# In a gated attention-plus-GLU kernel, the last down-projection job gets one PSUM bank for each half of the array, and the last PV block is issued later

## The chip, the cores and the metric

The kernel runs on one core of a Trainium2 chip. The metric is device time in microseconds (us) for one execution. The kernel before has a median of 1606.62 us over three runs (1606.62, 1606.66 and 1602.75).

## The reference

One input x of 2048 tokens by 512 features goes through two branches, which a gate mixes token by token:

```
x = A_x                                   # (1, 2048, 512), fp32
g = sigmoid((x * gate_w).sum(-1, keepdims=True))
# a: attention, 32 heads of 16, one shared K and one shared V of 16
q = (x @ wq) as (32 heads, 2048, 16);  k = x @ wk;  v = x @ wv
a = softmax(q k^T / 4) v, heads joined, @ wo          # (2048, 512)
# b: bilinear GLU with 1792 hidden units
b = ((x @ w_gate) * (x @ w_up)) @ w_down              # (2048, 512)
out = g * a + (1 - g) * b
```

## The kernel before

**Numbers.** Each fp32 operand of a projection is kept as a high and a low part, and a product is made as three matmuls: high by high, high by low, low by high (`mm3`). So the names come in pairs: `wdh`/`wdl` for w_down, `hh`/`hl` for the hidden units, `woh`/`wol` for wo, `oh`/`ol` for the normalised attention output.

**Lanes.** Nearly all matmuls of the main part contract over 64 rows of the array or fewer. Lane 0 works on rows 0 to 63, lane 1 on rows 64 to 127, and the two can run side by side. Scores for the maximum (`s1`, line 790) and for the exponential (`s2`, line 849) each use one lane; so do the job products (line 986): a job is one 128x512 output with 12 products, and each product has two halves, one for each lane. PV matmuls (`acc`, line 862) use all 128 rows and 32 columns each, in blocks. At the very end, 24 whole-array matmuls of 256 columns (`wo`, line 1151) finish the last token tile.

**Jobs.** A job is a piece of a projection: a query projection, a gate or up projection, a down projection, or the output projection wo of one token tile. Down and wo jobs add to `y`, the output tile in SBUF (`y_add`, line 399). In `fill`, the two lanes take a job's products one job apart: lane 0 does its 12 halves of job k while lane 1 does its 12 halves of job k-1. Without more, both lanes accumulate in the same PSUM bank, lane 0 first. Where nothing else has shown that lane 0's last write is done, lane 1 starts behind a `fence` (line 940): two tiny matmuls with two small VectorE copies, one after the other. A job with `apart` set gives each lane a bank of its own, and the two halves reach `y` in two adds. Before the change, `apart` is set for some down jobs and for the last but one wo job.

**Order of the work.** The instruction streams are written by a planner in Python. `State` (E) keeps a model of when each lane, bank, and engine is free. While scores are left, the token strings `ORDER` and `APART` set the order. When all maxima are done, `st["idle"]` becomes true; from there evacuations that went to ScalarE or GpSimd go to VectorE. The last stretch is made by `end_token`: it issues the remaining `s2` tokens, PV rounds (`token("p")`, a round takes two key blocks in four matmul instructions, which the profile records as eight) and job products. When all PV rounds are issued, the loop over `more(l)` empties the jobs, and the last loop (line 1151) writes the whole-array wo matmuls.

**The end of the attention.** After the last PV round ScalarE copies `acc` to `osb`; `o_last` then makes `sums` and `pick` on TensorE (line 742), VectorE makes a reciprocal and a product, and `oh`/`ol` for the last 128 columns are split off (lines 744, 746, 155, 156). The last six `wo` matmuls need them. `y_half` adds the two 256-column halves to `y` and starts the output transfers.

The tile names of the last stretch: `ms1_25566` is the last down job (token tile 15, hidden units 1024 to 1535), `ms0_25639` and `ms2_25687` (before) or `ms2_25641` and `ms1_25656` (changed) are the two lanes of the wo job of token tile 14, `acc_25458` is the last unit's PV accumulator.

Of the kernel before, what the change touches and what calls it, by code (L numbers as in the profile page):

```python
# [53 lines left out]
LASTORDER = 1000  # L54
SWAP = (10, 11, 12, 15)
LAT, LAT_LAST = 1.0, 0.5
LEADJOBS = 6
O0, O1 = 0, 0

# [18 lines left out]
def mix_kernel(ctx: ExitStack, tc: tile.TileContext, x, wq, wk, wv, wo, wg, wu, wd, gw, out):  # L78
# [50 lines left out]
    NS = NU * NJ  # L129
# [24 lines left out]
    def split(hi, lo, src):  # L154
        nc.scalar.copy(hi, src)
        nc.vector.tensor_sub(lo, src, hi.bitcast(F32))

    def mm3(a, b):
        return [(a[0], b[0]), (a[1], b[0]), (a[0], b[1])]
# [13 lines left out]
    def ms_bank(i):  # L173
        return bank(i, f"ms{i}")
# [21 lines left out]
    st = {"gen": None, "next": None, "q": 0, "tail": False, "idle": False, "apart": False, "picked": False}  # L196
# [198 lines left out]
    def y_add(c, t, p, gcol, n=1):  # L395
        start = clock["act"]
        own = yadd.get((c, t), -1e9)
        if (c, t) in y and (st["idle"] or ydue[0] > start + STALL and own < start + STALL):
            nc.vector.scalar_tensor_tensor(y[c, t], p, gcol, y[c, t], op0=OP.mult, op1=OP.add)
            end = spend("dve", 690.0, own)  # L400
        elif (c, t) not in y:
            y[c, t] = w512("y", F32, 8)
            ydone[c, t] = 0
            nc.scalar.activation(y[c, t], p, AF.Copy, scale=gcol)
            end = spend("act", COPY)
        else:
            tmp = w512("yt", F32, 2)
            nc.scalar.activation(tmp, p, AF.Copy, scale=gcol)  # L408
            end = spend("act", COPY, ydue[0])
            nc.gpsimd.tensor_tensor(y[c, t], y[c, t], tmp, op=OP.add)  # L410
            end = spend("pool", 1240.0, end)
            ydue.append(end)
            yadd[c, t] = end
        ydone[c, t] += n
        if ydone[c, t] == YADDS:
            done = y.pop((c, t))
            at(end + 200.0, lambda: nc.sync.dma_start(out2[c * 512 + t * 128:c * 512 + t * 128 + 128, :], done))

    class Job:


        def __init__(self, prods, evac, ready, p=None, start=True, parts=1):
            self.prods, self.evac, self.ready, self.p, self.start = prods, evac, ready, p, start
            self.parts, self.apart = parts, parts > 1
            self.end = self.items = self.len = None

    front, late = deque(), deque()
    jobs = {}
# [4 lines left out]
    def peek():  # L433

        while st["gen"] is not None and (st["next"] is None or st["next"].apart):
            if st["next"] is not None:
                late.append(st["next"])
            st["next"] = next(st["gen"], None)
            if st["next"] is None:
                st["gen"] = None  # L440
        if late and ready(late[0]) and (st["apart"] or st["idle"] or st["next"] is None):
            return late[0]
        if front and ready(front[0]) and (len(front) > 1 and not st["tail"] or not ready(st["next"])):
            return front[0]
        return st["next"] if ready(st["next"]) else None

    def take():
        j = peek()
        for jobs in (late, front):
            if jobs and j is jobs[0]:  # L450
                return jobs.popleft()
        st["next"] = None
        return j
# [152 lines left out]
    def down_jobs(c, fs, hat):  # L606
        n = FG // len(fs)
        for t in range(0, NT, n):
            def prods(t=t):
                return [m for i in range(t, t + n) for f in fs  # L610
                        for m in mm3((h[f][0][:, KS[i]], h[f][1][:, KS[i]]), wds[f])]

            def evac(p, i, halves=1, t=t):
                y_add(c, t + i, p, gb[:, c * NT + t + i:c * NT + t + i + 1], halves)
            yield Job(prods, evac, lambda: max(hat.get(f, 1e18) for f in fs), parts=n)

    def ffn_jobs():
        for c in range(NC):
# [136 lines left out]
    halves = {}  # L755
# [168 lines left out]
    E = State()  # L924
# [3 lines left out]
    jobs = {}  # L928
# [21 lines left out]
    def fill(l):  # L950

        c = count[l] + (O0, O1)[l]
        count[l] += 1
        k, i = c // 12 - l, c % 12
        wait = 0.0
        if i == 0 and l == 0:
            st["apart"] = apart and k % 3 == SLOT
            for _ in range(40):
                if peek():
                    break  # L960
                wait_ns(100.0)
            if peek():
                j = jobs[k] = take()
                j.items = j.prods()
                j.len = len(j.items) // j.parts
                j.end, j.bank, j.p = [[None, None] for _ in range(j.parts)], {}, {}
            st["apart"] = False
        j = jobs.get(k)
        if j is None or i >= len(j.items):
            return  # L970
        part, i = divmod(i, j.len)
        if i == 0 and (l == 0 or j.apart):
            b = E.claim()
            wait, E.free[b] = E.free[b], 1e18
            j.bank[part] = b
            j.p[part] = ms_bank(b)
            if j.apart:
                own[l] = b, j.p[part]
        elif i == 0 and j.end[part][0] > E.known:
            fence()  # L980
        b, p = own[l] if j.apart else (j.bank[part], j.p[part])
        at = E.issue(l, wait)
        E.wrote[b] = E.seq
        lhs, rhs = j.items[part * j.len + i]
        end = i + 1 == j.len
        nc.tensor.matmul(p, lhs[HALVES[l]], rhs[HALVES[l]], start=(i == 0 and (l == 0 or j.apart)),  # L986
                         stop=(end and (l == 1 or j.apart)))
        if end:
            j.end[part][l] = E.seq
            if part + 1 == j.parts and None not in j.end[part]:  # L990
                del jobs[k]
            if l == 1 or j.apart:
                clock["T"] = max(clock["T"], at)
                clock["act"], clock["dve"] = max(E.act, at + SEEN), max(E.dve, at + SEEN)
                if st["idle"]:
                    E.free[b] = clock["dve"] + RED_END + GAP
                    clock["act"] = E.act
                else:
                    E.free[b] = clock["act"] + COPY_END + GAP
                    clock["dve"] = E.dve  # L1000
                j.evac(p, part)
                E.act, E.dve = max(E.act, clock["act"]), max(E.dve, clock["dve"])
# [35 lines left out]
    def wait_ns(ns):  # L1038
        E.nl = [max(E.nl) + ns] * 2
        events_until(max(E.nl))  # L1040
# [20 lines left out]

    count = [-12 * LEADJOBS - O0, -12 * (LEADJOBS - 1) - O1]
    while min(E.n1) < LEAD or min(count) < 0:
        l = 0 if E.nl[0] <= E.nl[1] else 1
        k = E.n1[l]
# [8 lines left out]
    def ripe():  # L1074
        t, n = (E.last + PV_OUT if E.inpv else max(E.nl)) + RIPE, 0
        while all(E.ready.get((E.npv + n, v), (1e18,))[0] <= t for v in range(2)):
            n += 1
        return n // 2

    def end_token():  # L1080
        rounds = ripe()
        left2 = NS - min(E.n2)
        if rounds >= (BLOCK if left2 else 1) or rounds and not left2 and not any(map(fillable, range(2))):
            for _ in range(rounds):
                token("p")
            return
        now = E.last + PV_OUT if E.inpv else min(E.nl)
        for l in sorted(range(2), key=lambda l: (now if E.inpv else E.nl[l], E.n2[l])):
            for h in sorted(range(2), key=lambda h: E.n2[h]):
                k = E.n2[h]  # L1090
                if (l == (0 if swapped(k) else h) and k < NS and k - E.npv < PBUF and k <= E.n2[1 - h] + 1
                        and E.act < now + AHEAD and min(E.free) <= now + 100.0
                        and mat.get(k // NJ, 1e18) <= clock["T"] + 200.0):
                    return token("cd"[h] if h == l else "x")
            if fillable(l):
                return token("ef"[l])
            if not E.inpv and E.nl[l] < E.nl[1 - l]:
                break
        if rounds:
            return token("p")  # L1100
        if E.inpv:
            E.nl, E.inpv = [E.last + PV_OUT] * 2, False
        l = 0 if E.nl[0] <= E.nl[1] else 1
        E.nl[l] += 30.0
        events_until(min(E.nl))
# [22 lines left out]
    while jobs or more(0):  # L1128
        ls = [l for l in range(2) if more(l)] or [1]
        l = min(ls, key=lambda l: (E.nl[l], l))  # L1130
# [6 lines left out]
    while events or front or late or st["gen"] or st["next"]:  # L1137
        run_events()
        if peek():
            j = take()  # L1140
            items = j.prods()
            n = len(items) // j.parts
# [32 lines left out]
```

## Time and profile before

| what | value |
|---|---|
| median of three runs | 1606.62 us |
| the profiled execution's own time | 1608.26 us |
| its span, first to last instruction | 1606.3 us |
| TensorE (matmul) busy | 1600.6 us, 13157 matmuls |
| VectorE busy | 1338.6 us, 2424 instructions |
| ScalarE busy | 1203.4 us, 2360 instructions |
| GpSimd busy | 720.5 us, 858 instructions |
| mean granted TensorE clock | 0.995 |

All numbers but the first row's are from one execution. Busy shares are over the whole span; the change touches only its last part, so the views that count are those which can be narrowed to a stretch: the timeline, the windows with busy time and granted clock, and the chain of waits that ended last.

### The profile page before, as it was taken

The numbers are of one execution on the slowest core, as the hardware profiler recorded it, in microseconds if no ns is written. First come the engines' busy times: TensorE is split into PE (matmuls) and PEld (weight loads), VectorE is DVE, ScalarE is ACT, GpSimd is POOL, SyncE is SP. The second block draws the span as 40 slices with busy tenths as digits, with TensorE's granted clock in tenths as the row PEclk, the third lists the DMA queues.
The fourth block names the chain that finished last, engine by engine and source line by source line (L and its number), as shares of the span: only waits on it lengthen the run. The fifth ranks groups of instructions, "written<-read, shape, count | busy, mean of one in ns | idle before, by whom it ended". The sixth has DMA issues, their size and how long they took to land.

```text
span 1606.3 us, 35611 instructions
## 1 busy us (share of the span) xinstructions
PE 1600.6 (100%) x13157; PEld 1052.9 (66%) x13157; DVE 1338.6 (83%) x2424; ACT 1203.4 (75%) x2360; POOL 720.5 (45%) x858
## 2 busy tenths in 40 slices
PE   9999999999999999999999999999999999999998
PEld 8766666666666666666666666666666666666655
DVE  7988888888888888888888888888888888888862
ACT  4577778777788777777788777777778777777773
POOL 3334643525643642625444552544544542544520
PEclk9999999999999999999999999999999999999998
DMA  4563322212412222212232311212231221212101
GB/s 156 191 202 120 100 58 68 60 48 80 125 40 68 73 62 59 66 49 72 67 98 63 86 55 53 81 46 64 79 98 48 81 72 54 75 45 67 45 25 34
DMA packets 185557, 121.68 MB, mean 76 GB/s; under 512 B 46378, under 2 KB 154998, under 8 KB 185384
## 3 DMA queue, kind: packets, MB, share of 16 engines
q1 hardware_dynamic: 184176, 119.21, 24.9%
q8 instruction: 104, 1.70, 0.4%
q14 instruction: 69, 0.57, 0.1%
q10 hardware_dynamic: 1208, 0.20, 0.1%
HBM read 82.96 MB, written 36.17 MB: 74 GB/s over the span
## 4 chain that ended last, share of the span: by engine, by line
PE 100%; DVE 0%; DVEq 0%; issue 0%
PE ms L986 36%; PE acc L862 29%; PE s L790 17%; PE s L849 16%; PE ms L163 1%; PE px L298 0%; PE wo L1151 0%; PE px L283 0%; PE warm L875 0%; PE pv L341 0%; PE warm L878 0%; DVE y L772 0%; DVEq L1171 0%; PE sums L742 0%; PE pv L353 0%; PE fence L940 0%
## 5 line engine op out<-in xcount | busy, mean ns | idle before, releaser
L791 DVE TENSOR_REDUCE mx<-s 128x1 f32<-128x512 f32 x2048 | 1260.1, 681 | 205.1 <-PE s L849 130.7
L850 ACT ACTIVATE P<-s 128x512 f32<-128x512 f32 x2048 | 1067.9, 631 | 196.2 <-PE s L790 115.1
L849 PE MATMUL s<-Q,KK 50*128 50x512 f32 x2044 | 713.2, 405 | 0.0
L790 PE MATMUL s<-KK,Q 48*128 48x512 f32 x2048 | 711.1, 406 | 0.0
L862 PE MATMUL acc<-P,V 128*32 128x512 f32 x4096 | 480.1, 597 | 0.0
L790 PEld LDWEIGHTS s<-KK,Q 48*128 48x128 f32 x2048 | 347.5, 185 | 140.9 <-issue 43.8
L849 PEld LDWEIGHTS s<-Q,KK 50*128 50x128 f32 x2044 | 354.9, 185 | 84.7 <-issue 53.7
L986 PE MATMUL ms<-xh,wh 64*128 64x512 f32 x920 | 321.7, 394 | 0.0
L986 PE MATMUL ms<-xh,wl 64*128 64x512 f32 x920 | 321.3, 391 | 0.0
L986 PE MATMUL ms<-xl,wh 64*128 64x512 f32 x920 | 307.6, 391 | 0.0
L862 PEld LDWEIGHTS acc<-P,V 128*32 128x32 f32 x4096 | 113.4, 109 | 253.2 <-issue 232.5
L591 POOL TENSOR_TENSOR hf<-gs 128x512 f32<-128x512 f32 x56 | 72.1, 1288 | 371.9 <-ACT gs L582 360.8
L410 POOL TENSOR_TENSOR y<-y,yt 128x512 f32<-128x512 f32 x67 | 85.7, 1284 | 214.3 <-ACT yt L408 211.2
L986 PEld LDWEIGHTS ms<-xh,wh 64*128 64x128 f32 x920 | 161.4, 186 | 14.3 <-POOL wl L151 0.2
L986 PEld LDWEIGHTS ms<-xh,wl 64*128 64x128 f32 x920 | 159.2, 186 | 10.6
L986 PE MATMUL ms<-wdh,hh 64*128 64x512 f32 x448 | 161.1, 398 | 0.0
L986 PEld LDWEIGHTS ms<-xl,wh 64*128 64x128 f32 x920 | 153.9, 185 | 9.9
L986 PE MATMUL ms<-wdh,hl 64*128 64x512 f32 x448 | 159.4, 394 | 0.0
L986 PE MATMUL ms<-wdl,hh 64*128 64x512 f32 x448 | 156.7, 394 | 0.0
L151 POOL TENSOR_TENSOR wl<-wn,wh 128x512 fp32r<-128x512 f32 x117 | 151.0, 1290 | 9.4
L866 ACT COPY osb<-acc 128x512 f32<-128x512 f32 x64 | 37.6, 588 | 137.1 <-PE acc L862 137.1
L986 PEld LDWEIGHTS ms<-wdh,hh 64*128 64x128 f32 x448 | 80.1, 186 | 6.6 <-ACT P L850 0.4
(174 smaller groups left out, 1282.5 us busy)
## 6 DMA issues: line engine op xcount, KB each, us to landing
do<-osb SPq DMA_DIRECT2D x63, 256.0 KB
wn<-in_B_w_gate_dram SPq DMA_DIRECT2D x56, 256.0 KB
wn<-in_B_w_up_dram SPq DMA_DIRECT2D x56, 256.0 KB
wdn<-in_B_w_down_dram SPq DMA_DIRECT2D x56, 256.0 KB
Q<-dq SPq DMA_DIRECT2D x384, 32.0 KB
raw<-do SPq DMA_DIRECT2D x252, 32.0 KB
dq<-oh SPq DMA_DIRECT2D x16, 256.0 KB
dq<-ol SPq DMA_DIRECT2D x16, 256.0 KB
```

The lines of the kernel that those rows point to most:

```text
L151: nc.gpsimd.tensor_tensor(lo, src, hi.bitcast(F32), op=OP.subtract)
L163: nc.tensor.matmul(p, l, r, start=start and i == 0, stop=stop and i == len(prods) - 1)
L410: nc.gpsimd.tensor_tensor(y[c, t], y[c, t], tmp, op=OP.add)
L591: nc.gpsimd.tensor_tensor(hf, gu[0], gu[1], op=OP.mult)
L790: nc.tensor.matmul(p, q[r, slot], KK[r, kq * 512:(kq + 1) * 512], start=True, stop=True)
L791: nc.vector.tensor_reduce(mx[u][:, half * 4 + slot, kq:kq + 1], p, axis=AX.X, op=OP.max)
L849: nc.tensor.matmul(p, kj, q[r].rearrange("p s q -> p (s q)"), start=True, stop=True)
L850: nc.scalar.activation(P[s][:, half], p, AF.Exp, scale=0.25)
L862: nc.tensor.matmul(acc[u][b:b + 32, :], V[:, j + i], src[:, half], start=(j == 0), stop=(j == NJ - 2))
L866: nc.scalar.copy(osb, acc.pop(u))
L986: nc.tensor.matmul(p, lhs[HALVES[l]], rhs[HALVES[l]], start=(i == 0 and (l == 0 or j.apart)), stop=(end and (l == 1 or j.apart)))
```

## The change

It has two parts. First, a down job that is not split in parts gets a mark (`adds`). When lane 0 takes such a job after all score maxima are done, `split` turns it into an `apart` job: each lane then has its own bank, and each lane's sum is added to `y` by its own VectorE instruction, counted as half an add. Second, `end_token` holds back the PV round that would finish PV while more than `LATE` = 16 job products (halves, of both lanes) are left and a lane can be filled.

```
+import functools
...
+LATE = 16
...
             self.end = self.items = self.len = None
+            self.adds = False
+
+        def split(self):
+            if self.adds and not self.apart:
+                self.apart, self.adds = True, False
+                self.evac = functools.partial(self.evac, halves=0.5)
...
-            yield Job(prods, evac, lambda: max(hat.get(f, 1e18) for f in fs), parts=n)
+            j = Job(prods, evac, lambda: max(hat.get(f, 1e18) for f in fs), parts=n)
+            j.adds = n == 1
+            yield j
...
                 j.len = len(j.items) // j.parts
+                if st["idle"]:
+                    j.split()
...
+    def todo():
+        n = 0
+        for k, j in jobs.items():
+            for l in range(2):
+                n += max(0, len(j.items) - max(0, count[l] - 12 * (k + l)))
+        return n + 24 * (sum(j.p is None for j in (*front, *late)) + (st["next"] is not None))
+
     def end_token():
         rounds = ripe()
         left2 = NS - min(E.n2)
+        more = not left2 and E.npv + 2 * rounds >= NS and todo() > LATE and any(map(fillable, range(2)))
+        if more:
+            rounds = 0
         if rounds >= (BLOCK if left2 else 1) or rounds and not left2 and not any(map(fillable, range(2))):
```

The instruction streams of ScalarE, GpSimd and SyncE keep their rows and order. On TensorE everything up to the last down job's seventh lane-0 product is the same row for row; on VectorE everything up to the add of `ms2_25577`.

TensorE, at the place where the last PV block stood before the change. `ms1_25566` is the last down job, `acc_25458` the PV accumulator, `ms0_25639` lane 0 of the wo job of token tile 14:

```order
L986 MATMUL ms2_25577<-wdl_24919,hh_24913 128x512
L986 MATMUL ms1_25566<-wdh_24121,hh_24116 128x512
L986 MATMUL ms1_25566<-wdh_24121,hl_24117 128x512
L862 MATMUL acc_25458<-P_25601,V_91 32x512 x2
L862 MATMUL acc_25458<-P_25610,V_91 32x512 x2
L986 MATMUL ms1_25566<-wdl_24122,hh_24116 128x512
L986 MATMUL ms1_25566<-wdh_24416,hh_24411 128x512
L986 MATMUL ms1_25566<-wdh_24416,hl_24412 128x512
L986 MATMUL ms1_25566<-wdl_24417,hh_24411 128x512
L986 MATMUL ms0_25639<-woh_98,oh_24779 128x512
L742 MATMUL sums_25641<-osb_25633,sel1_24136 32x128 x4
```

The same place in the changed kernel; `ms3_25628` is lane 1 of the last down job, in its own bank:

```order
L998 MATMUL ms2_25577<-wdl_24919,hh_24913 128x512
L998 MATMUL ms1_25566<-wdh_24121,hh_24116 128x512
L998 MATMUL ms3_25628<-wdh_22971,hh_22966 128x512
L998 MATMUL ms1_25566<-wdh_24121,hl_24117 128x512
L998 MATMUL ms3_25628<-wdh_22971,hl_22967 128x512
L998 MATMUL ms1_25566<-wdl_24122,hh_24116 128x512
L998 MATMUL ms3_25628<-wdl_22972,hh_22966 128x512
L998 MATMUL ms1_25566<-wdh_24416,hh_24411 128x512
```

Lane 1 of that job starts here, alternating in the program with lane 0, and the PV block is gone from this place.

TensorE again, before the change, where lane 1 of the last down job begins (twelve products of `ms1_25566` follow the fence, then twelve of `ms2_25687`, lane 1 of the wo job, then the 24 of `wo`):

```order
L986 MATMUL ms0_25639<-woh_98,ol_24780 128x512
L986 MATMUL ms0_25639<-wol_99,oh_24779 128x512
L940 MATMUL fence_25667<-ident_70 32x32 x2
L986 MATMUL ms1_25566<-wdh_22971,hh_22966 128x512
L986 MATMUL ms1_25566<-wdh_22971,hl_22967 128x512
```

In the changed kernel this is the end of that job's lane 1 and the new place of the PV block; `ms2_25641` and `ms1_25656` are lanes 0 and 1 of the wo job:

```order
L998 MATMUL ms3_25628<-wdl_24417,hh_24411 128x512
L998 MATMUL ms2_25641<-woh_98,oh_24779 128x512
L998 MATMUL ms1_25656<-woh_98,oh_24779 128x512
L872 MATMUL acc_25458<-P_25601,V_91 32x512 x2
L872 MATMUL acc_25458<-P_25610,V_91 32x512 x2
L998 MATMUL ms2_25641<-woh_98,ol_24780 128x512
L998 MATMUL ms1_25656<-woh_98,ol_24780 128x512
```

The fence is gone, and PV now stands behind 24 more products than before. Behind it come 16 job products ahead of `wo`: four for each lane, then `sums` and `pick`, then one more for lane 0 and seven for lane 1.

VectorE, from the add of `ms2_25577` on, before:

```order
L399 SCALAR_TENSOR_TENSOR y_21795<-ms2_25577,gb_93,y_21795 128x512
L744 RECIPROCAL rb_25651<-sums_25641 128x128
L746 TENSOR_TENSOR oT_24714<-pick_25642,rb_25651 128x128
L156 TENSOR_TENSOR ol_25595<-oT_24714,oh_25594 128x128
L941 COPY ft_25668<-fence_25667 32x32 x2
L399 SCALAR_TENSOR_TENSOR y_21701<-ms0_25639,gg_92,y_21701 128x512
L399 SCALAR_TENSOR_TENSOR y_21795<-ms1_25566,gb_93,y_21795 128x512
L772 SCALAR_TENSOR_TENSOR y_21795<-wo_25700,gg_92,y_21795 128x256
```

And in the changed kernel:

```order
L401 SCALAR_TENSOR_TENSOR y_21795<-ms2_25577,gb_93,y_21795 128x512
L401 SCALAR_TENSOR_TENSOR y_21795<-ms1_25566,gb_93,y_21795 128x512
L401 SCALAR_TENSOR_TENSOR y_21795<-ms3_25628,gb_93,y_21795 128x512
L754 RECIPROCAL rb_25682<-sums_25672 128x128
L756 TENSOR_TENSOR oT_24714<-pick_25673,rb_25682 128x128
L158 TENSOR_TENSOR ol_25595<-oT_24714,oh_25594 128x128
L401 SCALAR_TENSOR_TENSOR y_21701<-ms2_25641,gg_92,y_21701 128x512
L782 SCALAR_TENSOR_TENSOR y_21795<-wo_25695,gg_92,y_21795 128x256
```

The two fence copies are gone, the last down job's add has become two, and both stand ahead of the reciprocal. Behind these rows, both kernels have the second `y_21701` add and the second `y_half` add.

## The prediction

> **What bounds the kernel now.** The page's chain of work that ended last, narrowed to the last 26 us, comes first: start, length, and what the time went to.
>
> ```profile
> 1580.73 0.99 PE acc L862 x8
> ...
> 1583.66 2.69 PE ms L986 x11
> ...
> 1586.95 10.35 PE ms L986 x24
> 1597.30 4.26 PE wo L1151 x21
> ...
> 1601.59 0.48 DVE y L772
> ```
>
> TensorE alone sets the end. After the last PV block it needs 20 us, and half of that is one row: 24 job products of 64 rows, after the fence, with nothing of the other lane left. Then 21 `wo` matmuls, the first `y_half`, and 4.71 us to the span's end at 1606.3. Since rows before the split are identical in both programs, only what lies behind 1580.10 us counts.
>
> Next the windows. Columns: length, busy us and count for TensorE, weight loads, VectorE, ScalarE, GpSimd; then granted TensorE clock, DMA share, GB/s.
>
> ```profile
> 1200.00:1580.10 380.10, 380.10 (x3158) 243.90 (x3155) 308.81 (x558) 295.34 (x581) 162.20 (x196) 1.00 0.20 57
> 1580.10:1583.60 3.50, 3.50 (x34) 1.58 (x31) 0.84 (x2) 0.96 (x2) 0.00 (x0) 1.00 0.00 0
> 1583.60:1587.10 3.50, 3.23 (x18) 2.34 (x15) 1.74 (x6) 0.30 (x1) 0.00 (x0) 1.00 0.00 0
> 1587.10:1600.80 13.70, 13.70 (x41) 10.85 (x40) 1.48 (x3) 0.00 (x0) 0.00 (x0) 0.50 0.00 1
> 1600.80:1601.60 0.80, 0.80 (x8) 0.80 (x8) 0.01 (x1) 0.00 (x0) 0.00 (x0) 1.00 0.00 0
> ```
>
> The granted clock is 1.00 all along, falls to 0.50 for 13.7 us exactly in this stretch, and comes back some 3.5 us after the whole-array `wo` matmuls begin. It falls after 3.5 us that hold hardly anything but products on half the rows, and the fence. The stretch before it, with fewer such products plus a PV block, kept 1.00.
>
> The timeline gives the steps (start to start; columns: start, duration, engine, line, what).
>
> ```profile
> 1583.92 0.39 PE L986 MATMUL ms<-wol,oh 64*128 64x512 f32 x1
> ...
> 1585.96 0.39 PE L986 MATMUL ms<-wol,oh 64*128 64x512 f32 x1
> ...
> 1586.75 0.20 PE L940 MATMUL fence<-ident 32*32 32x32 f32 x1 [0.27 <-DVE ft L941]
> 1586.88 0.61 PE L986 MATMUL ms<-wdh,hh 64*128 64x512 f32 x1
> 1587.29 0.62 PE L986 MATMUL ms<-wdh,hl 64*128 64x512 f32 x1
> ...
> 1596.68 0.62 PE L986 MATMUL ms<-wol,oh 64*128 64x512 f32 x1
> 1597.23 0.58 PE L1151 MATMUL wo<-woh,oh 128*128 128x256 f32 x1
> 1597.61 0.41 PE L1151 MATMUL wo<-woh,ol 128*128 128x256 f32 x1
> ...
> 1600.38 0.41 PE L1151 MATMUL wo<-wol,oh 128*128 128x256 f32 x1
> ...
> 1600.91 0.28 PE L1151 MATMUL wo<-wol,oh 128*128 128x256 f32 x1
> ...
> 1601.27 0.28 PE L1151 MATMUL wo<-wl,oh 128*128 128x256 f32 x1
> ...
> 1601.62 0.28 PE L1151 MATMUL wo<-wl,oh 128*128 128x256 f32 x1
> ```
>
> A lone product at full clock: nine steps from 1583.92 to 1585.96, 0.227 us each. At half clock: 22 steps from 1587.29 to 1596.68, 0.427. A `wo` step: 13 from 1597.61 to 1600.38, 0.213; six from 1600.91 to 1601.62, 0.118, taken as 0.119. The fence puts 0.92 us between two products (1585.96 to 1586.88).
>
> Two lanes side by side:
>
> ```profile
> 1574.70 0.40 PE L986 MATMUL ms<-wdh,hl 64*128 64x512 f32 x1
> 1574.71 0.40 PE L986 MATMUL ms<-wdh,hh 64*128 64x512 f32 x1
> 1574.94 0.40 PE L986 MATMUL ms<-wdl,hh 64*128 64x512 f32 x1
> 1574.95 0.39 PE L986 MATMUL ms<-wdh,hl 64*128 64x512 f32 x1
> ```
>
> Two products start within 0.01 us, and the next two 0.24 later: a pair costs what a lone product costs.
>
> **The change, step by step.** These rows price the switches between kinds of matmul:
>
> ```profile
> 1580.10 0.40 PE L986 MATMUL ms<-wdh,hh 64*128 64x512 f32 x1
> 1580.34 0.39 PE L986 MATMUL ms<-wdh,hl 64*128 64x512 f32 x1
> 1580.66 1.06 PE L862 MATMUL acc<-P,V 128*32 128x512 f32 x8
> 1581.65 0.49 PE L986 MATMUL ms<-wdl,hh 64*128 64x512 f32 x1
> 1581.99 0.39 PE L986 MATMUL ms<-wdh,hh 64*128 64x512 f32 x1
> ...
> 1582.69 0.39 PE L986 MATMUL ms<-woh,oh 64*128 64x512 f32 x1
> 1583.02 0.42 PE L742 MATMUL sums<-osb,sel 128*32 128x128 f32 x8
> ...
> 1583.59 0.49 PE L986 MATMUL ms<-woh,ol 64*128 64x512 f32 x1
> ```
>
> The product at 1580.10 is the last row that both programs share. Before, 41 more products follow it, all lone: 41 steps. Now they stand as 1 (partner of the shared row), 12 pairs, PV, 4 pairs, `sums` and `pick`, 1 pair, 6 lone: 23 steps. From 1580.10 on, in us:
>
> - 12 pair steps of 0.24: 2.88; pair to PV, as 1580.34 to 1580.66: 0.33
> - PV: 0.99; first pair step behind it, as 1581.65 to 1581.99, 0.34, and two of 0.24: 0.82
> - to `sums`: 0.33; `sums` and `pick` until the next product (1583.02 to 1583.59): 0.57
> - pair to first lone product 0.34, five steps of 0.227: 1.14; to `wo`: 0.33
> - first `wo` step 0.25; 19 more to the 21st: 2.26; 21st to `y_half` (1601.27 to 1601.59): 0.32
>
> Sum 10.56, against 1601.59 - 1580.10 = 21.49 before: **10.93 us less**. By causes: 18 steps fewer at 0.227 is 4.1; the fence 0.92 - 0.227 = 0.7; the clock 24 x 0.20 = 4.8 on products and 17 x 0.094 = 1.6 on `wo`; pairs 0.2 dearer.
>
> Three terms have no row at this clock. Lone product to `wo`: from 0.227 (an ordinary step) to 0.55 (1596.68 to 1597.23 at half clock); I take 0.33, nearest to the full-clock switches. First `wo` step: from 0.119 to 0.38 (half clock); 0.25, the middle. Lane 1's new bank is number 3, which ScalarE reads last in the fourth of the five exponentials below, so until about 1577.92 + 4/5 x 2.56 = 1579.97; I take no wait, and 0.4 (all five) as the other end. Pairs may also cost 0.227. Together -0.4 to +0.8 us.
>
> **What hides the rest.** PV moves 2.7 us later, and with it the chain that feeds the last six `wo` matmuls:
>
> ```profile
> 1577.92 2.56 ACT L850 ACTIVATE P<-s 128x512 f32<-128x512 f32 x5 [0.91 <-PE s L849]
> ...
> 1580.30 0.75 DVE L399 SCALAR_TENSOR_TENSOR y<-ms,gb,y 128x512 f32<-128x512 f32 x1 [1.58 <-PE ms L986]
> ...
> 1581.87 0.59 ACT L866 COPY osb<-acc 128x512 f32<-128x512 f32 x1 [1.39 <-PE acc L862]
> ...
> 1583.51 0.96 DVE L744 RECIPROCAL rb<-sums 128x128 f32<-128x128 f32 x1 [2.45 <-PE sums L742]
> ...
> 1585.22 0.29 DVE L156 TENSOR_TENSOR ol<-oT,oh 128x128 fp32r<-128x128 f32 x1 [0.36 <-ACT oh L155]
> ```
>
> PV now starts at 1583.31. The copy `osb` ends 1.80 behind PV's start (1580.66 to 1582.46), so at 1585.11; `sums` comes at 1585.45: 0.3 us of cover, the thinnest, lost one for one. `ol` is ready 2.49 behind `sums` (1583.02 to 1585.51): 1587.94. The first `wo` that needs it, the 19th, stands at 1590.10: 2.2 us of cover. This chain is what comes next if TensorE gets shorter still.
>
> On VectorE the two adds ahead of the reciprocal take 0.75 each. The first ends near 1582.5 (lane 0 done at 1581.7); the wo job's second bank, which waits for it, is wanted at 1582.98. The second ends near 1583.9, 1.5 us before `sums`. So the extra add, the only added instruction, costs nothing; behind a TensorE pause of 0.5 us the first would cost what is missing. No DMA is added or moved past another on any queue; the last adds and transfers keep their order, so the 4.71 us at the end stay.
>
> **The clock** is the one large assumption: that it stays at 1.00. The thinnest 3.5 us of the new order holds `sums` and `pick` (0.57), six lone products (1.5), and otherwise pairs, PV or `wo`. The window 1580.10 to 1583.60 had more lone products (seven) with the same `sums`, and kept 1.00.
>
> [...]
>
> **The time.** The profiled execution took 1608.26 us (span 1606.3 and 1.96 around it): 1608.26 - 10.93 = 1597.3. The median of the runs lies 1.64 below it. If that is the price of profiling, the runs give 1595.7; if it is a smaller loss to the clock in those runs (one of them is 3.9 us shorter than the others), it goes with the loss, and they give 1597.3. I take the middle, **1596.5 us**, 0.6% below 1606.62.
>
> [...]
>
> **Rivals.**
>
> 1. *The clock falls in the new tail too.* Against it: the stretch that kept 1.00. For it: the cause of the fall was inferred from one case. Half clock from the lone products on costs 6 x 0.20 + 24 x 0.094 = 3.5: 1600.8. Chance 0.10.
> 2. *The clock falls as early as the PV block.* All from PV on doubles: 10.56 - 2.88 - 0.33 - 0.32 = 7.0 more, 1604.4. Chance 0.05.
> 3. *Slower: the lanes take turns.* If lanes 0 and 1 of these jobs, in their two banks, run one after the other, the array is half filled from 1580.10 on and the clock falls from there. The 18 pairs then cost 0.454 instead of 0.24, 3.9 more; (10.56 - 0.32 + 3.9) x 2 + 0.32 = 28.6 against 21.49: 1615.4. At half clock it decides from a pair step of 0.259 on (on the full-clock scale). Against it: the four rows of pairs above. Chance 0.02.
>
> That the change doesn't do what it says is no rival: the rows in the program show both parts.
>
> **How the numbers follow.** My forecast has 0.83. Its own range is 1595.3 (1595.7 - 0.4) to 1598.1 (1597.3 + 0.8). Runs of this kernel scatter by 3.9 us, so I go down to 1593.5, and up to 1600.8 to take in rival 1. Measurement can tell about 0.3%, 4.8 us, from no change, so faster means below 1601.8: forecast and rival 1, 0.93. Within 0.3%: rival 2, 0.05. Slower: 0.02.
>
> **What would show it.** In the changed profile: granted clock 1.00 until the last `wo`; 13 pairs 0.24 apart from 1580.10; PV near 1583.3, `sums` near 1585.4, the first `wo` near 1587.8 with steps of 0.119; the first `y_half` near 1590.7 and a span of 1595.4. VectorE's reciprocal must wait for `sums`, not for its adds. Wrong if the clock row reads 0.50 anywhere behind 1583, if pairs are 0.45 apart, or if the 19th `wo` waits for `ol`.

## The result and the profile after

| | before | changed |
|---|---|---|
| median of four runs each | 1606.59 us (1602.75 to 1606.66) | **1597.19 us** (1596.88 to 1597.58) |
| ratio of the times | | 0.9947, 95% interval 0.9930 to 0.9965 |
| profiled execution: time, span | 1608.26, 1606.3 us | 1597.58, 1595.6 us |
| mean granted clock | 0.995 | 0.999 |

The kernel is 9.4 us faster by the medians and 10.7 by the two profiled executions.

First the chain of work that ended last, in the changed kernel, from the end of the last ordinary PV block on (start, length, what the time went to; DVEq is VectorE's sequencer, and that row spans the second add of the wo job):

```profile
1580.23 3.47 PE ms L998 x28
1583.70 0.99 PE acc L872 x8
1584.70 1.12 PE ms L998 x8
1585.82 0.36 PE sums L752 x8
1586.18 0.22 PE pick L752 x8
1586.40 1.81 PE ms L998 x7
1588.21 2.72 PE wo L1173 x21
1590.93 0.03 issue
1590.96 0.48 DVE y L782
1591.44 0.66 DVEq L1193
1592.10 0.39 DVE y L782
```

TensorE still sets the end. The row of 24 lone products that took 10.35 us before is gone: the products now stand in rows of 28, 8 and 7. The 21 `wo` matmuls take 2.72 us where they took 4.26.

The windows of the same stretch (length; busy us and count for TensorE, weight loads, VectorE, ScalarE, GpSimd; granted clock; DMA share; GB/s):

```profile
1580.10:1583.60 3.50, 3.50 (x32) 3.12 (x28) 1.59 (x3) 0.79 (x2) 0.00 (x0) 1.00 0.00 0
1583.60:1587.10 3.50, 3.50 (x38) 1.87 (x37) 1.52 (x2) 0.59 (x1) 0.00 (x0) 1.00 0.02 5
1587.10:1588.00 0.90, 0.90 (x5) 0.55 (x3) 0.43 (x3) 0.30 (x1) 0.00 (x0) 1.00 0.00 0
1588.00:1589.00 1.00, 1.00 (x8) 0.86 (x8) 0.92 (x2) 0.00 (x0) 0.00 (x0) 1.00 0.00 0
1589.00:1590.50 1.50, 1.50 (x15) 1.50 (x14) 0.00 (x0) 0.00 (x0) 0.00 (x0) 1.00 0.00 0
```

The clock column reads 1.00 in every row; the 13.7 us at 0.50 have no counterpart, and TensorE's busy time equals the length in each row.

The timeline, for the steps and the covers (start, duration, engine, line, what; in brackets the idle time ahead and what ended it):

```profile
1580.50 0.44 PE L998 MATMUL ms<-wdh,hh 64*128 64x512 f32 x2
1580.73 0.45 PE L998 MATMUL ms<-wdh,hl 64*128 64x512 f32 x2
...
1583.25 0.46 PE L998 MATMUL ms<-woh,oh 64*128 64x512 f32 x2
...
1583.63 1.06 PE L872 MATMUL acc<-P,V 128*32 128x512 f32 x8
...
1584.79 0.59 ACT L876 COPY osb<-acc 128x512 f32<-128x512 f32 x1 [3.90 <-PE acc L872]
...
1585.76 0.43 PE L752 MATMUL sums<-osb,sel 128*32 128x128 f32 x8
...
1586.25 0.96 DVE L754 RECIPROCAL rb<-sums 128x128 f32<-128x128 f32 x1 [1.98 <-PE sums L752]
...
1587.97 0.29 DVE L158 TENSOR_TENSOR ol<-oT,oh 128x128 fp32r<-128x128 f32 x1 [0.36 <-ACT oh L157]
...
1588.14 0.39 PE L1173 MATMUL wo<-woh,oh 128*128 128x256 f32 x1
...
1588.37 0.28 PE L1173 MATMUL wo<-woh,ol 128*128 128x256 f32 x1
...
1590.39 0.28 PE L1173 MATMUL wo<-wh,oh 128*128 128x256 f32 x1
...
1590.63 0.28 PE L1173 MATMUL wo<-wl,oh 128*128 128x256 f32 x1
```

Most pairs come as one row "x2", 0.23 us behind each other (between 1581.89 and 1583.09, left out here, the rows of the two lanes stand 0.06 us apart): a pair at the price of a lone product (0.227). From 1580.50, the product that both programs share, the first `y_half` (1590.96 in the chain) is 10.46 us away, where it was 21.49. VectorE has been idle for 1.98 us when `sums` comes, so the adds ahead of the reciprocal cost nothing.

### The profile page after: what moved, and what is told of

Read it like the earlier page. It is cut to its first block, busy times and chain, and to the rows that moved or that the text cites. A ratio compares the mean times of both kernels' runs of the same rounds, so it can differ in the third digit from the quotient of the medians.

```text
span 1595.6 us, 35607 instructions
## 1 busy us (share of the span) xinstructions
PE 1590.0 (100%) x13155; PEld 1046.0 (66%) x13155; DVE 1339.5 (84%) x2423; ACT 1203.5 (75%) x2360; POOL 719.5 (45%) x858
## 4 chain that ended last, share of the span: by engine, by line
PE 100%; DVE 0%; DVEq 0%; issue 0%
PE ms L998 36%; PE acc L872 29%; PE s L800 17%; PE s L859 16%; PE ms L165 1%; PE px L300 0%; PE px L285 0%; PE wo L1173 0%; PE warm L885 0%; PE pv L343 0%; PE warm L888 0%; DVE y L782 0%; DVEq L1193 0%; PE sums L752 0%; PE pv L355 0%
```

## The experiments

Ten further versions (7 is the changed kernel again) were run in three batches (1 to 4, 5 to 8, 9 and 10), each with runs of the kernel before beside them. A ratio is to the kernel before of the same batch.

| kernel | median us (lowest to highest, runs) | ratio, 95% | mean granted clock |
|---|---|---|---|
| 1 the split alone | 1597.70 (1597.42-1597.93, 4) | 0.9950 [0.9932, 0.9967] | .999-1.0 |
| 2 the hold alone | 1601.29 (1601.04-1602.08, 10) | 0.9969 [0.9959, 0.9978] | .999-1.0 |
| 3 before, lone products given a partner | 1601.51 (1601.14-1601.88, 10) | 0.9975 [0.9964, 0.9986] | .999-1.0 |
| 4 changed, plus 24 lone products | 1601.94 (1) | | .999 |
| 5 before's order without the fence | 1604.95 (1604.55-1606.25, 10) | 0.9997 [0.9985, 1.0009] | .996-.998 |
| 6 as 4, plus a fence among them | 1604.53 (1602.36-1606.00, 10) | 0.9992 [0.9980, 1.0005] | 1.0 in 3, .997-.999 in 7 |
| 7 changed, again | 1596.73 (1596.63-1596.84, 4) | 0.9941 [0.9919, 0.9962] | 1.0 |
| 8 changed, one add earlier | 1596.35 (1596.06-1596.57, 4) | 0.9938 [0.9921, 0.9956] | 1.0 |
| 9 as 5, without its wait | 1600.89 (1600.39-1601.25, 5) | 0.9963 [0.9949, 0.9978] | 1.0 |
| 10 PV held to the very end | 1597.85 (1597.49-1598.14, 4) | 0.9941 [0.9927, 0.9956] | .999-1.0 |

The kernel before was run 46 times in these batches, and its times fall into three groups by the clock that each run was granted: 11 runs at 1600.91 to 1602.47 (median 1601.61, clock 1.0), 18 at 1605.68 to 1607.11 (median 1606.14, clock .996 to .997), 17 at 1607.39 to 1608.54 (median 1607.71, clock .995 to .996). So the half clock comes in 35 runs of 46; that the two upper groups are two lengths of it is an estimate from their distance of 1.6 us, as only a run of the uppermost was traced. **1601.6 us is what the kernel before takes where its clock holds**. The batches aren't all at one level: these runs have medians of 1601.60, 1601.49 and 1602.34 in the first, second and third. The first two can be compared with each other; kernels 9 and 10 are read against 1602.34. The changed kernel took 1596.73 in the second batch (kernel 7), beside 1597.19 in its first runs.

### 1. The split alone (e1_split_only)

```
-LATE = 16
+LATE = 10**9
```

The last PV round goes out as early as before; the banks of the two lanes stay apart.

> Only the first part of the change: the last down job gets a bank for each lane; the last PV block is not held back. Its tail has the same number of steps as the changed kernel's: 18 pairs and 6 lone products, only with PV 12 pairs earlier. My sum gives the hold no term of its own, so it expects the time of the changed kernel within 0.5 us (span 1595.1 to 1596.1, granted clock 1.00 until the last wo). Rival, the hold is needed (to keep the lanes paired or the clock up): at least 2 us longer than the changed kernel, or a granted clock of 0.50 somewhere behind 1583 us.

The timeline of this kernel, around the wo job's start:

```profile
1582.75 0.96 DVE L754 RECIPROCAL rb<-sums 128x128 f32<-128x128 f32 x1 [2.07 <-PE sums L752]
...
1584.55 0.39 PE L998 MATMUL ms<-woh,oh 64*128 64x512 f32 x1
...
1584.68 1.59 DVE L401 SCALAR_TENSOR_TENSOR y<-ms,gb,y 128x512 f32<-128x512 f32 x2
...
1585.47 0.50 PE L998 MATMUL ms<-woh,oh 64*128 64x512 f32 x1 [0.54 <-DVE y L401]
```

The split alone keeps the clock and nearly all of the gain. What it lacks is one wait: with PV early the reciprocal and what follows it run from 1582.75 on, the two adds of the down job come only behind them, and lane 1 of the wo job waits 0.54 us for the bank that the first add frees. From the shared product to the first `y_half` it takes 11.52 us, 1.06 more than the changed kernel, and its median is 0.97 above that of kernel 7. **The hold is worth about 1.0 us**, more than the 0.5 that was allowed for and less than the rival's 2; what it does is to put the adds ahead of the reciprocal. The wait of 0.54 us, among pairs, didn't lower the clock in these four runs (.999 to 1.0).

### 2. The hold alone (e2_hold_only)

```
-                if st["idle"]:
-                    j.split()
```

> Only the second part: PV is held until 16 products are left, but the last down job keeps one bank. All 41 products behind the shared one stay lone and the fence stays; 17 lone products now stand in a row ahead of PV. Theory that half-filled work lowers the clock: it falls within about 4 to 7 us of 1580, earlier than in the kernel before, and stays low through the fence and 24 lone products: 0 to 5 us slower than the kernel before. Rival, the fence's gap lowers the clock: full clock until the fence near 1586, then as before: within 1 us of the kernel before. Neither expects a gain.

The windows ahead of the last PV block, over the fence, and behind it:

```profile
1579.70:1584.20 4.50, 4.50 (x24) 3.39 (x20) 0.75 (x1) 0.69 (x2) 0.00 (x0) 1.00 0.00 0
1585.20:1585.80 0.60, 0.32 (x6) 0.17 (x2) 0.18 (x1) 0.35 (x1) 0.00 (x0) 1.00 0.00 0
1585.80:1592.30 6.50, 6.50 (x41) 4.65 (x41) 2.47 (x5) 0.53 (x2) 0.00 (x0) 1.00 0.01 3
```

Neither theory had this. All 41 products are lone here, and the fence is there, yet the clock holds in all ten runs (.999 to 1.0), and the time is that of the kernel before with its clock held (1601.29 against 1601.61). What differs from before is only the place: 17 lone products stand ahead of PV, and the fence comes right behind PV (1585.24 and 1584.24), five lone products ahead of `sums` (1587.20), where the kernel before has 11 lone products between `pick` and the fence and 24 behind it. That this is why the clock holds is not shown. The lone products by themselves, 17 in a row ahead of PV (3.9 us) and 19 in a row behind `pick` (4.5 us), didn't lower the clock in these runs.

### 3. Before, with a partner for each lone product (e3_before_partner)

```
+        st["made"] = lhs, rhs
...
+    partner = bank(hold(), "partner")
...
+        st["made"] = None
         fill(l)
+        if st["made"] is not None:
+            lhs, rhs = (x[HALVES[1 - l]] for x in st["made"])
+            nc.tensor.matmul(partner, lhs, rhs, start=True, stop=True)
```

The first line stands in `fill`, the others at the loop over `more(l)`: behind the last PV round each lone product gets the other lane's half beside it, into a bank that nobody reads; nothing else changes, and the fence stays.

> The kernel before, but each lone product behind the last PV block has a partner: the other lane computes its half of the same product into a spare bank that nobody reads. The fence and its gap stay, the number of steps stays at 41; only the fill of the array changes. Half-filled work is the cause: granted clock 1.00 through the tail, first y_half 15.7 us behind the shared product instead of 21.5, span near 1600.5. The fence's gap is the cause: clock 0.50 from about 1587 for over 10 us all the same, span 1606 or more.

Windows ahead of the fence, over it, and behind it:

```profile
1581.10:1585.80 4.70, 4.70 (x52) 3.22 (x49) 1.54 (x3) 0.88 (x2) 0.00 (x0) 1.00 0.00 0
1585.80:1586.40 0.60, 0.33 (x4) 0.18 (x2) 0.18 (x1) 0.00 (x0) 0.00 (x0) 1.00 0.00 0
1586.40:1592.00 5.60, 5.60 (x49) 4.42 (x48) 1.59 (x3) 0.00 (x0) 0.00 (x0) 1.00 0.01 3
```

More work in the same places makes the kernel 0.25% faster: the clock holds in all ten runs (.999 to 1.0). So the fence's gap alone didn't lower it either; with lone products in the same places, as in the kernel before, it fell in 35 runs of 46. The step count is that of before, and so the time is that of before with its clock held.

### 4. The changed kernel plus 24 lone products (e4_after_lone24)

```
+        st["made"] = lhs, rhs
...
+    lone = bank(hold(), "lone")
+    lhs, rhs = (x[HALVES[1]] for x in st["made"])
+    for _ in range(24):
+        nc.tensor.matmul(lone, lhs, rhs, start=True, stop=True)
```

They stand ahead of `wo`, in a bank that nobody reads, behind the six lone products that the changed kernel has there.

> The changed kernel with 24 more lone products of lane 1, into a spare bank that nobody reads, between the last job product and the first wo; no fence and no gap. 24 x 0.227 = 5.4 us at full clock. Half-filled work is the cause: 30 lone products in a row (6.8 us) bring the clock to 0.50 before they end, and the time grows by 7 to 11 us against the changed kernel. The gap is the cause: clock 1.00 throughout and 5.4 us more.

```profile
1585.60:1592.50 6.90, 6.90 (x32) 5.34 (x29) 1.80 (x4) 0.30 (x1) 0.00 (x0) 1.00 0.01 2
```

In this window some 30 products of 64 rows follow each other without a gap, almost 7 us, and the clock stays at 1.00. The theory that half-filled work lowers the clock, taken alone, fails here, in one run (mean clock .999); kernels 2 and 9 agree, in fifteen runs (.999 to 1.0). From the shared product (1579.46) to the first `y_half` (1595.37) it takes 15.91 us, 5.45 more than the changed kernel, where 24 steps at full clock would be 5.4.

### 5. Before's order without the fence (e5_lone_nofence)

```
+                self.apart, self.adds, self.alone = True, False, True
...
+        if l == 1 and j is not None and j.alone and fillable(0):
+            return False
```

On top of kernel 1, lane 1 of the last down job waits until lane 0 has nothing left: in the program the lone products stand as before, but in their own bank, with no fence. Kernel 3 had the fence between pairs, kernel 4 lone products without a gap, and both kept the clock; the theory on trial is that the two lower it together.

> The kernel before in its order of TensorE work (PV early, then 41 lone products), but lane 1 of the last down job writes a bank of its own, so the fence and its gap go; its sum takes one more add on VectorE. [...] It expects 1.00 in every run, and 1601.0 us: the runs of the kernel before that kept the clock (1601.3 to 1602.2) less 0.7 for the fence. Rival, the order of before does it without the fence (36 lone products around sums and pick): clock 0.995 to 0.997 in most runs, 1605 to 1607 us.

```profile
1583.00:1587.40 4.40, 4.40 (x27) 3.63 (x23) 1.54 (x4) 0.30 (x1) 0.00 (x0) 1.00 0.00 0
1587.40:1589.30 1.90, 0.40 (x2) 0.00 (x0) 1.41 (x2) 0.00 (x0) 0.00 (x0) 1.00 0.00 0
1589.30:1590.80 1.50, 1.50 (x6) 1.22 (x7) 0.00 (x0) 0.00 (x0) 0.00 (x0) 0.98 0.06 11
1590.80:1597.50 6.70, 6.70 (x25) 5.61 (x24) 0.00 (x0) 0.00 (x0) 0.00 (x0) 0.50 0.00 0
```

The run did not test what it was meant to: the second row shows a new gap, 1.9 us in which TensorE is busy for 0.40 and VectorE's adds hold the bank that is wanted (the next product waits 1.50 us for them). The clock falls to 0.50 behind it in this trace, and the mean clock is .996 to .998 in all ten runs. The theory expected 1.00 in every run, for a kernel without such a gap. Taken by itself this can't separate the lone products from the gap; together with kernel 4 it suggests that both are needed, and kernels 6 and 9 try that from both sides. It does show that the gap need not be a fence: no transposes stand in these 1.9 us.

### 6. The fence put back among lone products (e6_lone24_fence)

```
+    gap, seen = bank(hold(), "fence"), work.tile([128, 32], F32, name="ft", bufs=2)
-    for _ in range(24):
+    for i in range(24):
+        for _ in range(2 * (i == 12)):
+            nc.tensor.transpose(gap[:32, :32], ident[:32, :32], ident[:32, :32])
+            nc.vector.tensor_copy(seen[0:32, :], gap[:32, :32])
```

Kernel 4, with a fence between its 12th and 13th added product. By the same theory the clock should fall here.

> The changed kernel with 24 lone products ahead of wo, as in the earlier run, but a fence (two small transposes, each waiting for the VectorE copy of the one before) stands in their middle. [...]

Windows ahead of the fence, over it, and from the fall on:

```profile
1587.00:1589.80 2.80, 2.80 (x13) 2.05 (x12) 0.27 (x1) 0.00 (x0) 0.00 (x0) 1.00 0.01 3
1589.80:1590.50 0.70, 0.43 (x4) 0.20 (x3) 0.18 (x1) 0.00 (x0) 0.00 (x0) 1.00 0.00 0
...
1591.00:1597.50 6.50, 6.50 (x20) 5.03 (x20) 0.43 (x1) 0.00 (x0) 0.00 (x0) 0.50 0.00 0
```

The one thing added to kernel 4 is the fence, and now the clock falls: to 0.50 in the trace, and to a mean of .997 to .999 in seven runs of ten (1603.99 to 1606.00), while three keep it (1.0, 1602.36 to 1602.91, median 1602.59, 0.65 above kernel 4). This agrees with the theory, and it also reproduces what the kernel before does, some runs with the fall (35 of 46 there) and some without.

### 7 and 8. The changed kernel again, and with one add earlier (e7_after_again, e8_add_early)

```
-                    at(clock["T"] + (2500.0 if E.npv == NS else 0.0),
+                    at(clock["T"],
```

In the changed kernel the second add of the wo job of tile 14 stands between the two adds of `y_half` (the 0.66 us in the chain). Kernel 8 issues it ahead of both.

> The changed kernel again, beside the next one on the same chip. All theories expect 1596.9 to 1597.6 us and a clock of 1.00 or 0.999.

> The changed kernel, but the second add of the wo job of token tile 14 is issued when its products end, ahead of the first y_half, where it stood between the two y_half adds. The add takes 0.66 us off the chain behind the last wo, if that chain sets the end: 0.5 to 0.8 us shorter than the changed kernel. Rival, the end is set by the output transfers: no difference.

VectorE's rows of kernel 8: the second wo add now goes together with the first, and the two adds of `y_half` follow each other.

```profile
1587.43 1.60 DVE L401 SCALAR_TENSOR_TENSOR y<-ms,gg,y 128x512 f32<-128x512 f32 x2
...
1590.22 0.88 DVE L782 SCALAR_TENSOR_TENSOR y<-wo,gg,y 128x256 f32<-128x256 f32 x2 [1.18 <-PE wo L1173]
```

The issue of the last output transfer, in kernel 7 and then in kernel 8 (ScalarE's queue):

```profile
1591.87 0.39 ACTq L784 DMA_DIRECT2D out_dram<-y  x1
```

```profile
1591.12 0.39 ACTq L784 DMA_DIRECT2D out_dram<-y  x1
```

The 0.66 us are gone from the chain, and the kernel is 0.38 us shorter by the medians, less than the 0.5 to 0.8 expected; the ranges of the two, from one batch, don't overlap. Kernel 7 lies just below the range expected for it, 1596.63 to 1596.84. The transfer is issued 0.75 us earlier, but the span ends only 0.3 us earlier (1594.7 and 1595.0). Why less is left behind that issue in kernel 7 (3.1 us against 3.6) is open; it is 3.6 again in kernel 10, whose trace has that add early too. This is the shortest version run, shorter than both kernels.

### 9. Lone products without any gap (e9_lone_nogap)

```
-            b = E.claim()
+            b = E.free.index(min(E.free)) if E.npv == NS and l else E.claim()
```

Kernel 5, but lane 1's jobs at the end claim the bank that has been free longest, so that none of them waits for an add.

> The run with lone products in the order of before and no fence, once more, but lane 1's products of the last two jobs go to banks that have been free longest, so that TensorE does not wait 1.5 us for VectorE's adds in the middle of the lone products. Same 41 lone products, now with no gap among them. Theory of lone products and gap together: clock 1.00 (or 0.999) in every run, 1600.5 to 1601.5 us, all within 1 us of each other. Rival, lone products in this order are enough: clock 0.995 to 0.998 in most runs, 1604 us or more.

```profile
1584.00:1588.00 4.00, 4.00 (x35) 3.23 (x36) 1.98 (x4) 0.30 (x1) 0.00 (x0) 1.00 0.00 0
1588.00:1592.00 4.00, 4.00 (x19) 3.00 (x18) 1.41 (x2) 0.00 (x0) 0.00 (x0) 1.00 0.02 4
```

TensorE is busy through both windows, and the clock is 1.00 in all five runs: the work of kernel 5, less its wait, kept the clock. But it isn't quite "the same 41 lone products":

```profile
1586.21 0.50 PE L998 MATMUL ms<-wdh,hh 64*128 64x512 f32 x1
1586.43 0.39 PE L998 MATMUL ms<-woh,oh 64*128 64x512 f32 x1
1586.55 0.39 PE L998 MATMUL ms<-wdh,hl 64*128 64x512 f32 x1
1586.66 0.39 PE L998 MATMUL ms<-woh,ol 64*128 64x512 f32 x1
```

In the program lane 1's products (`wdh` and `wdl` here) stand behind all of lane 0's (`woh` and `wol`). In the trace, with no fence between them, the first three run beside the last three of lane 0, here and in kernel 5 (lane 1 at 1584.78, 1585.11 and 1585.34 there, lane 0 at 1584.99, 1585.22 and 1585.45), which leaves 21 in a row ahead of `wo` and saves three steps. Against the kernel before with its clock held in the same batch (two runs) it is 1602.34 - 1600.89 = 1.4 us faster: the three steps (3 x 0.227 = 0.7) and the fence (0.92 - 0.227 = 0.7). The run doesn't price the fence by itself.

### 10. PV held until no job product is left (e10_pv_last)

```
-LATE = 16
+LATE = 0
```

> The changed kernel, but PV is held until no product is left (LATE = 0). Nothing then covers the copy of acc on ScalarE: sums cannot start before 1.9 us behind PV's start, so TensorE stands still for about 0.8 us between PV and sums, while the last six wo products still find ol ready. 0.3 to 0.9 us longer than the changed kernel, 1597.1 to 1597.7; clock 1.00 or 0.999, since PV and wo fill the array around the gap. Rival, the chain behind sums is then late at the 19th wo: over 1 us longer. Rival, any gap behind lone products lowers the clock: 0.998 or less and 1599 us or more.

```profile
1587.72 0.43 PE L752 MATMUL sums<-osb,sel 128*32 128x128 f32 x8 [0.73 <-ACT osb L876]
```

Held too long, the copy `osb` has no cover: TensorE waits 0.73 us between PV and `sums`. The stretch from the shared product takes 10.79 us in place of 10.46, and the median is 1597.85. The wait thus costs less than its length; probably because PV no longer stands among the pairs, which saves changes between kinds of matmul (in the changed kernel 0.38 us from a pair to PV, 1583.25 to 1583.63, and 0.34 from the first pair behind PV to the next, 1584.63 to 1584.97, where a pair step is 0.23; not tried by itself). The median is 0.15 us above the range expected, in a batch that lies some 0.8 us above the others, so it can't say more. The rival that any gap behind lone products lowers the clock fell: the clock is .999 to 1.0 in all four runs.

One experiment wasn't tried: the kernel before without its fence and with nothing in its place. Both lanes write one bank there, and nothing else orders them. Kernel 9 took away the reason for the fence instead.

## Why the prediction was right, and where it wasn't

**The sum.** Shared product to first `y_half`, term by term:

| term | predicted us | measured us |
|---|---|---|
| 12 pair steps | 2.88 | 2.75 |
| to PV, and PV | 1.32 | 1.38 |
| four pairs, to `sums` | 1.15 | 1.13 |
| `sums` and `pick` | 0.57 | 0.57 |
| to the lone products, and five steps | 1.48 | 1.50 |
| to `wo`, and its first step | 0.58 | 0.54 |
| 19 `wo` steps, to `y_half` | 2.58 | 2.59 |
| sum | 10.56 | 10.46 |

The tail is thus 21.49 - 10.46 = 11.03 us shorter; the two executions differ by only 10.7, since the shared product itself came 0.40 us later (1580.50 and 1580.10), behind rows that are the same in both. What follows the first `y_half` stayed, as forecast: 4.64 us in place of 4.71. The 0.1 us comes from the pairs (0.229 a step, the lone product's price, in place of 0.24). The three terms that had no row came out at 0.31 (lone product to `wo`), 0.23 (first `wo` step) and no wait for the new bank: near the values chosen, far from the ends.

**The covers** were right. `osb` ended at 1585.38, 0.38 us ahead of `sums` (predicted 0.3); kernel 10 shows that this cover is needed. `ol` was ready at 1588.26, 2.1 us ahead of the 19th `wo` (predicted 2.2). By its row (1590.39) the 19th reads `oh`; the first that reads `ol` is the 20th, so this cover is 0.1 us larger still.

**By causes**, over the runs of the second batch, which has both kernels, rather than in one execution: the clock is worth 1606.2 - 1601.5 = 4.7 us of the median, since not every run loses as much to it as the profiled one (6.4 predicted there, and 1607.7 - 1601.5 = 6.2 in the group of runs to which it belongs). Pairing and the fence are worth 1601.5 - 1596.7 = 4.8, where 4.1 + 0.7 - 0.2 = 4.6 was forecast; the pairs weren't 0.2 dearer. The fence's share of 0.7 is read from rows (0.92 - 0.227), and kernels 4 and 6, with 0.65 between them, agree.

**First miss: the base.** "I take the middle" between 1595.7 and 1597.3 was 0.7 us too low. The 1.64 us between the profiled execution and the median was not a price of profiling: where the clock held, the profiled execution of a kernel lies within 0.4 us of that kernel's median (1597.58 and 1597.19 for the changed one). It was the second reading, a smaller loss to the clock: the step between the two upper groups is 1607.71 - 1606.14 = 1.6. With that, 1597.3 stands against 1597.19 measured. Kernel 7, at 1596.73, looks nearer to the middle, but the kernel before was lower in that batch too: the gain is 9.4 us in the one and 9.5 in the other, where the middle stands for 10.1 and the second reading for 9.3.

**Second miss: the cause of the fall.** The prediction judged the new tail by its lone products: six in its thinnest stretch, seven in one that kept 1.00. That is only half of it. Kernels 4 and 9 have 30 and 21 lone products in a row and keep the clock; kernel 3 has the fence between pairs and keeps it; kernel 6 has both and loses it in seven runs of ten, and kernel 5, with a longer gap, in ten of ten. **In these runs lone products lowered the clock together with a gap among them; neither was enough alone.** In the kernel before both lie within the 3.5 us ahead of the fall (1583.60 to 1587.10). The forecast held because the change takes away both; as far as the cause goes, that was luck. Kernel 2 would have been misjudged by the prediction's reason: by its 41 lone products alone it should lose the clock, and it kept it in ten runs of ten.

**Third: the hold had no term.** The prediction counted PV's new place only as a risk to covers. The hold has a gain of its own, about 1.0 us, since it puts two adds ahead of the reciprocal and so frees a bank in time (kernel 1). The sum came out without such a term because it priced the finished order, in which no bank is waited for.

The rivals: the granted clock is 1.00 down to the last `wo`, so neither 1 nor 2 came about; pairs 0.229 us apart rule out 3.

## What to carry to other kernels

A tail in which only half of the array worked was dear through its number of steps (18 more, 4.1 us here), and dearer still where a short wait (0.92 us between two products) stood among them and the clock fell (some 6 us in the longest runs); taking away either the half-filled steps (kernel 3, ten runs) or the wait (kernel 9, five runs) kept the clock. Read times that fall into groups by the granted clock of each run before a gap between the profiled execution and the median is put down to anything else. And when a step is moved on the engine that sets the end, look at which small instructions of the next engine it moves past: a bank that came free late cost 1 us in kernel 1.

## What the runs showed of the hardware

The clock fell to 0.50 without any long idle time. In the 3.5 us ahead of the fall in the kernel before (1583.60 to 1587.10), TensorE is idle for 0.27 us, all of it inside the fence, and the longest distance between two products is 0.92; yet 35 of 46 runs fell. The same fence between pairs (kernel 3) or right behind PV (kernel 2) lowered nothing in ten runs each; half-filled products without a gap lowered nothing in the one run with some 7 us of them (kernel 4) and in the five with some 5 us (kernel 9). Behind the longer gap of 1.9 us among them (kernel 5) the clock fell in ten runs of ten.

The half clock lasted 13.7 us in the profiled execution of the kernel before and some 6.8 in those of kernels 5 and 6 (windows of 6.7 and 6.5 us at 0.50, with neighbours at 0.98 and 0.95, and at 0.91). Half-filled products, though without a gap from 1586.88 to 1597.23, didn't bring it back in the kernel before; in the three executions it came back 2.4 to 4.1 us after the first whole-array `wo`.

The two lanes need not start in the order of the program: without a fence between them, lane 1 started at 1584.78 in kernel 5, ahead of three products of lane 0 that precede it there (1584.99 to 1585.45), and at 1586.21 in kernel 9, ahead of lane 0's at 1586.43 and 1586.66.

Kernels 3 and 6 show that it counts whether pairs or lone products stand around the gap: the fall came in none of ten runs with pairs and in seven of ten with lone products. Pairs differ from lone products in how full the array is; that this is what counts, how it is weighed against the idle time, and why some runs of one kernel fell and others didn't, is not shown here: no run moved the gap by itself.
